# The second layer of whole expert blocks as seven block products, over halves of tokens, features and outputs

## The chip, the cores and the metric

The kernel runs on one core of a Trainium2 chip. The metric is the device time of one execution, in microseconds. Before the change it is 2567.09 us, the median of three runs from 2567.05 to 2567.15.

## The reference

An attention unit without a softmax, and behind it a layer of eight experts in which a hash of the token's number picks the expert. Everything is in float32.

```
B, S, D = 8, 2496, 256;  d_qk = 64;  N = B * S = 19968;  E, F = 8, 1024
scores = z @ z.T / S                      # per batch
x = (u * (maximum(scores, 0)**2 @ v)).reshape(N, D)
e = token_ids * 2654435761 % E            # the expert of each row
h = maximum(x @ w1[e], 0)                 # first layer, 256 -> 1024
out = h @ w2[e]                           # second layer, 1024 -> 256
```

## The kernel before

The first 1510 us or so are the attention; the change does not touch them. There each gated row of x is also stored to its slot in DRAM, where the rows of one expert stand together. What follows is the expert part, and all line numbers here are those of the kernel before.

The slots are cut into 32 **whole blocks** of 512 rows, each of one expert, and 31 **small blocks**: 27 of 128 rows of one expert, and 4 made of halves of 64 rows, three of them with two experts' weights and one, the lone half, with one. The list `work` (line 1066) takes them in turn: whole, small, whole, small, ..., and a whole one at the end. `run` (line 1016) goes through this list in steps; the program's order is written out by hand and each engine takes its instructions in that order. At step i it does the first layer of block i, and somewhere within it the second layer of block i - 1. There are two calls of `run`, since near the end a branch stands that is taken only when rows must be done again; the first call ends behind a small block.

*First layer of a whole block* (`ups_mixed`, line 872, for all but the first block; that one uses `ups`). It computes h transposed: 1024 features on partitions, 512 tokens in columns. It uses Winograd's form of Strassen's method: the weights w1 are cut into 2x2 parts over the two halves of the 256 inputs and of the 1024 features, x into 2x2 parts over inputs and tokens, and seven products of mixed parts take the place of eight. The four mixed parts of w1 (`mix_w`, line 855, s1 to s4 in `w_mix`) are made by GpSimd, the four of x (`mix_x`, line 865) by VectorE, both ahead of the block. Each product is done for two halves d of its features in PSUM banks; sums that are needed twice are copied out by ScalarE (`kept`, line 898) into one of five buffers `rest`, taken in turn, and added by VectorE (`total`, line 904); the rectification of these sums is a GpSimd instruction behind it (line 906). One of the four parts comes rectified out of PSUM by ScalarE (line 934). The eight `yield`s let `run` put other work between the pieces: at k = 1 the next small block's x is turned (`turn_x`), at k = 6 the second layer of the small block before is done.

*First layer of a small block* (`ups_of_part`, line 948): two steps of one PSUM bank each, with the tokens on partitions; ScalarE rectifies the first bank (line 944), VectorE the second (line 946), and 16 transposes on VectorE turn the result (line 982).

*Second layer* (`down`, line 984). For each 128 tokens of block i - 1 one PSUM tile of 128x256 is the sum of eight matmuls (stationary: 128 features by 128 tokens of h; moving: 128 features by 256 outputs of w2). ScalarE copies it to the SBUF (line 1005), and GpSimd issues an indirect store to the tokens' rows (line 1010). For a whole block that is four such tiles, 32 matmuls. They all stand in the second step (k = 1) of the small block's first layer, with `mix_w` for the next whole block between the second and the third of them:

```
                    for n in range(-(-len(do) * 2 // (len(banks) - k + 1))):
                        if n == 2 and work[i] >= NW:
                            mix_w(work[i + 1])
                        do.pop(0)()
```

Ahead of them in that step, and so ahead of them on VectorE, stand the rectification of the second bank, and `turn_x` and `mix_x` of the next whole block. A float32 matmul of the program stands in the trace as two records (MATMUL), each with its own weight load (LDWEIGHTS); a transpose by TensorE as one. The time from the start of one whole block to the start of the next is called a period below.

## Time and profile before

| what | value |
|---|---|
| median of 3 runs | 2567.09 us |
| the profiled execution's own time | 2569.34 us |
| its span, first to last instruction | 2567.6 us |
| TensorE busy | 2556.2 us |
| VectorE, ScalarE, GpSimd busy | 1541.3, 656.4, 1042.9 us |
| instructions | 28507 |
| granted clock of TensorE, mean | 1.000 |

Three things help to read it. The busy share is of the whole span, while the change lies in the part from about 1550 us on, so the stretches there are looked at by themselves. In the list of groups the mean is the time from an instruction's start to its end; matmuls and loads overlap with what follows, so the distance between two starts is found in the rows in order of time, as the length of a row of many minus one instruction's own, divided by their number less one. And a row in order of time gives in square brackets how long the engine had been idle before it, and who ended that.

### The profile page before, as it was taken

What the parts mean: (1) busy time and instruction counts of PE and PEld (TensorE: products, weight loads), DVE (VectorE), ACT (ScalarE), POOL (GpSimd) and SP (SyncE); (2) the same over time, 40 slices, a digit from 0 to 9 for tenths busy, and PEclk for the clock granted to TensorE, in tenths of its full rate; (3) what the DMA queues carried; (4) which work ended last, traced back from release to release, by engine and by line L of the source; (5) the groups of instructions that cost most, each with busy time, mean ns of one, the idle gap of its engine ahead of it and who ended that gap; (6) DMA issues with size and microseconds to landing.
All of it is one profiled execution on the core that took longest, in us unless ns stands there. A gap on an engine that the chain in (4) does not pass through costs nothing.

```text
span 2567.6 us, 28507 instructions
## 1 busy us (share of the span) xinstructions
PE 2556.2 (100%) x8827; PEld 1581.7 (62%) x8827; DVE 1541.3 (60%) x3441; ACT 656.4 (26%) x1392; POOL 1042.9 (41%) x980
## 2 busy tenths in 40 slices
PE   9999999999999999999999999999999999999999
PEld 4444444444444444444454457888888888888887
DVE  7976767767758758757856835444444444444443
ACT  5215204214223222232233102222222222222212
POOL 1342332332233133133231225555555555556555
PEclk9999999999999999999999999999999999999999
DMA  4442343343333333433423359667668668667651
GB/s 123 123 122 64 96 110 83 79 108 88 85 97 98 84 93 93 90 96 86 115 69 79 82 148 249 166 168 197 166 163 198 172 168 202 173 167 175 168 134 52
DMA packets 445531, 322.99 MB, mean 126 GB/s; under 512 B 267292, under 2 KB 408237, under 8 KB 445376
## 3 DMA queue, kind: packets, MB, share of 16 engines
q1 hardware_dynamic: 423456, 279.38, 44.7%
q0 software_dynamic: 20624, 41.09, 5.0%
q8 instruction: 72, 1.18, 0.2%
q14 instruction: 83, 0.68, 0.1%
q10 hardware_dynamic: 1296, 0.66, 0.1%
HBM read 231.19 MB, written 66.81 MB: 116 GB/s over the span
## 4 chain that ended last, share of the span: by engine, by line
PE 97%; issue 1%; POOL 1%; DVE 0%; POOLq 0%; ACT 0%; DVEq 0%
PE acc L362 50%; PE o_ps L991 20%; PE h_ps L889 14%; PE s_ps L235 7%; PE h_ps L976 4%; PE acc L370 2%; PE h_ps L844 1%; POOL out_dram L1010 1%; POOL hT L906 0%; DVE hT L982 0%; PE warm L655 0%; PE z_ps L179 0%; PE h_ps L957 0%; POOL u_sb L860 0%; POOL u_sb L861 0%
## 5 line engine op out<-in xcount | busy, mean ns | idle before, releaser
L362 PE MATMUL acc<-a,v_sb 128*128 128x512 f32 (+1 forms) x1760 | 765.9, 592 | 0.0
L273 DVE STREAM_TRANSPOSE m<-a 32x512 f32<-32x512 f32 (+1 forms) x896 | 603.9, 674 | 18.9 <-ACT a L251 3.6
L362 PEld LDWEIGHTS acc<-a,v_sb 128*128 128x128 f32 x1760 | 342.2, 196 | 390.5 <-issue 377.5
L362 PE MATMUL acc<-m,v_sb 128*128 128x512 f32 (+1 forms) x1280 | 527.5, 571 | 1.8 <-issue 1.8
L398 POOL TENSOR_TENSOR x_sb<-x_sb,u_sb 128x256 f32<-128x256 f32 (+1 forms) x156 | 108.3, 723 | 912.7 <-DMA x_sb<-x_way 912.7
L243 ACT ACTIVATE a<-s_ps 128x512 f32<-128x512 f32 (+3 forms) x456 | 202.1, 582 | 1036.3 <-PE s_ps L235 976.9
L362 PEld LDWEIGHTS acc<-m,v_sb 128*128 128x128 f32 x1280 | 251.1, 196 | 273.8 <-issue 271.0
L991 PE MATMUL o_ps<-m,hT 128*128 128x256 f32 (+1 forms) x1904 | 414.1, 379 | 0.0
L991 PEld LDWEIGHTS o_ps<-m,hT 128*128 128x128 f32 (+1 forms) x1904 | 353.8, 188 | 61.0 <-issue 12.5
L906 POOL TENSOR_SCALAR hT<-hT 128x512 f32<-128x512 f32 x186 | 275.1, 1496 | 96.0 <-DVE hT L905 95.0
L299 DVE STREAM_TRANSPOSE a<-a 32x128 f32<-32x128 f32 (+2 forms) x1360 | 282.3, 240 | 9.9
L1010 POOL DMA_INDIRECT out_dram<-o_sb,idx x155 | 156.3, 1009 | 320.6 <-ACT o_sb L1005 298.0
L905 DVE TENSOR_TENSOR hT<-stage,h_ps 128x512 f32<-128x512 f32 x112 | 77.0, 688 | 259.7 <-PE h_ps L889 245.5
L251 ACT ACTIVATE a<-a 128x512 f32<-128x512 f32 (+1 forms) x480 | 229.5, 639 | 0.0
L378 DVE STREAM_TRANSPOSE x_q<-acc 128x512 f32<-128x512 f32 (+1 forms) x80 | 56.7, 708 | 284.2 <-PE acc L362 281.4
L982 DVE STREAM_TRANSPOSE hT<-hT 32x256 f32<-32x256 f32 x480 | 209.0, 435 | 6.3
L1005 ACT COPY o_sb<-o_ps 128x256 f32<-128x256 f32 x158 | 58.9, 373 | 553.9 <-PE o_ps L991 553.9
L235 PE MATMUL s_ps<-zT 64*128 64x512 f32 (+1 forms) x960 | 188.7, 536 | 0.0
L889 PE MATMUL h_ps<-x_sb,u_sb 128*128 128x256 f32 x744 | 185.9, 379 | 0.0
L640 POOL DMA_INDIRECT x_rows<-x_sb,slot_i x160 | 157.2, 982 | 69.7 <-issue 36.7
L628 POOL DMA_INDIRECT slot_tokens<-token,addr x160 | 155.3, 971 | 50.8 <-issue 48.1
L235 PEld LDWEIGHTS s_ps<-zT 64*128 64x128 f32 x960 | 111.7, 186 | 93.8 <-issue 64.7
(156 smaller groups left out, 1810.9 us busy)
## 6 DMA issues: line engine op xcount, KB each, us to landing
m<-in_moe_w_dram SPq DMA_DIRECT2D x200, 256.0 KB
m<-in_moe_w_dram SPq DMA_DIRECT2D x50, 1024.0 KB
m<-stage SPq DMA_DIRECT2D x320, 64.0 KB
v_sb<-in_v_dram SPq DMA_DIRECT2D x32, 512.0 KB
u_sb<-in_u_dram SPq DMA_DIRECT2D x32, 512.0 KB
x_way<-x_q SPq DMA_DIRECT2D x128, 128.0 KB
x_sb<-x_way SPq DMA_DIRECT2D x32, 512.0 KB
v_sb<-x_rows SPq DMA_DIRECT2D x128, 128.0 KB
```

The source lines that it names most:

```text
L235: nc.tensor.matmul(ps[:, lo:n], zT[b][h, ts(t, P)], zT[b][h, ds(g * G * P + lo, n - lo)], start=True, stop=True)
L243: nc.scalar.activation(a, ps[:, lo:n], AF.Relu)
L251: nc.scalar.activation(a, a, AF.Square, scale=1.0 / S)
L273: nc.vector.transpose(o, x[ts(r, Q), 0:m * G, ts(c, Q)].rearrange("p (i s) q -> p i s q", s=G))
L299: return n * Q, lambda: nc.vector.transpose(out, in_)
L362: nc.tensor.matmul(acc[h][:, 0:queries(g)], v_sb[b][:, t, h::2], squares(b, g, t), start=(k == 0), stop=(k == TM - 1), skip_group_check=True)
L640: st = nc.gpsimd.indirect_dma_start(out=x_dram[:, :], out_offset=bass.IndirectOffsetOnAxis(ap=slot_i[0:width(c % T), c:c + 1], axis=0), in ...
L889: nc.tensor.matmul(ps[:, ts(i, W)], terms[k][0][:, ts(2 * d + i, P)], terms[k][1], start=first and i == 0, stop=True, skip_group_check=True)
L906: nc.gpsimd.tensor_scalar_max(o, o, 0.0)
L982: nc.vector.transpose(turned[ts(c, Q), :, ts(r, Q)], rows[ts(r, Q), :, ts(c, Q)])
L991: nc.tensor.matmul(ps[cols, :], hT[j][f][:, ts(t, P)][:, cols], w[:, f, :], start=(f == 0), stop=(f == n - 1), skip_group_check=True)
L1010: st = nc.gpsimd.indirect_dma_start(out=out[:], out_offset=bass.IndirectOffsetOnAxis(ap=rows, axis=0), in_=o, in_offset=None, bounds_check ...
```

## The change

The second layer of every whole block but the first is done by `downs_mixed`, again with seven products of Winograd's form. The left operand is h, cut into halves of tokens and of features; the right one is w2, cut into halves of features and of outputs. Each product is 256 tokens by 512 features by 128 outputs: eight matmuls with 128 columns, four parts of features for each of two token tiles. Products 2 and 5 or 3 share a PSUM bank; products 1, 6, 7 and 4 go to the other and add up there. ScalarE copies out three partial sums and the last part, VectorE adds the other three parts from PSUM into a whole output block (`o_blocks`), and the stores go out two at a time, behind product 3 and behind product 4.

The mixed parts of w2 are four differences on GpSimd (`mix_w2`), those of h four per half d on VectorE (`mix`), two of them with the rectification of one operand folded in. The other three parts of h are rectified in place by ScalarE (`rectify`), and GpSimd no longer rectifies. In `run`, products 1, 2, 5 and 6 stand behind the first step of the small block's first layer, products 7, 3 and 4 behind its second; `mix_w` for the next whole block keeps its condition n == 2, which now is ahead of product 4 and its stores. Two buffers of `rest` move to a new pool, since their room is taken by the mixed parts of w2.

```diff
@@ -815,6 +815,8 @@
     o_all = vpool.tile([P, T, D], F32, name="v_sb")
     nc.gpsimd.memset(o_all[:, 0:BLK // P * AHEAD + (MH - NH + 2) // 2, :], 0.0)
     xT_buf.append(turned_x(o_all, T // XW - 1))
+    assert BLK // P * AHEAD + (MH - NH + 2) // 2 <= 2 * BLK // P and T // XW > 4
+    o_blocks = [o_all[:, ts(k, BLK // P), :] for k in (2, 3)]
     w_free.append(len(w_buf))
     w_buf.append([npool.tile([P, T, NQ, Q], F32, name="zn")[:].rearrange("p t j k -> p (t j k)")[:, 0:DP * F],
@@ -850,7 +852,10 @@
     x_mix = xpool.tile([P, G, D], F32, name="x_sb")[:].rearrange("p g (k i) -> p g k i", i=Q)
     rest = [spool.tile([P, BLK], F32, name="stage")[:] for _ in range(3)]
-    rest += [xpool.tile([P, G, D], F32, name="x_sb")[:].rearrange("p g d -> p (g d)")[:, ts(k, BLK)] for k in range(2)]
+    w2_mix = [xpool.tile([P, G, D], F32, name="x_sb")[:].rearrange("p g (k d) -> p (g k) d", k=2),
+              qpool.tile([P, G * NQ, D // NQ], F32, name="x_q")[:].rearrange("p (k n) d -> p k (n d)", k=8)]
+    w2_mix = [w2_mix[k // 2][:, ts(k % 2, 4)] for k in range(4)]
+    rest += [opool.tile([P, BLK], F32, name="kept", bufs=2)[:] for _ in range(2)]
     def mix_w(j):
@@ -861,6 +866,16 @@
         nc.gpsimd.tensor_sub(s2, s1, a11)
         nc.gpsimd.tensor_sub(s3, a11, a21)
         nc.gpsimd.tensor_sub(s4, a12, s2)
+    def mix_w2(j):
+        w = w2[j][0]
+        (b11, b12), (b21, b22) = ([w[:, ts(k, FP // 2), ts(c, P)] for c in range(2)] for k in range(2))
+        t1, t2, t3, t4 = w2_mix
+        nc.gpsimd.tensor_sub(t1, b12, b11)
+        nc.gpsimd.tensor_sub(t2, b22, t1)
+        nc.gpsimd.tensor_sub(t3, b12, b22)
+        nc.gpsimd.tensor_sub(t4, b21, t2)
     def mix_x(j):
@@ -903,7 +918,21 @@
         def total(o, a, c):
             nc.vector.tensor_add(o, a, bank(c))
-            nc.gpsimd.tensor_scalar_max(o, o, 0.0)
+        def rectify(r, c, d):
+            o = part(r, c, d)
+            nc.scalar.activation(o, o, AF.Relu)
+        mixes = [apool.tile([P, 2, G, W], F32, name="hS", tag="a") for _ in range(2)]
+        h_mix[j] = [tiles[0][:, :, 0:W], tiles[1][:, :, 0:W], tiles[1][:, :, W:], *(m[:, k] for m in mixes for k in range(2))]
+        def mix(d):
+            a11, a12, a22, s1, s2, s3, s4 = (m[:, ts(d, 2)] for m in h_mix[j])
+            a21 = part(0, 1, d)
+            nc.vector.scalar_tensor_tensor(s1, a21, 0.0, a22, op0=OP.max, op1=OP.add)
+            nc.vector.tensor_sub(s2, s1, a11)
+            nc.vector.scalar_tensor_tensor(s3, a21, 0.0, a11, op0=OP.max, op1=OP.subtract)
+            nc.vector.tensor_sub(s4, a12, s2)
         begun = []
         sums = [[mm_ps.tile([P, BLK], F32, name="h_ps", tag="mm") for _ in range(3)] for _ in range(2)]
@@ -933,11 +962,75 @@
             times(d, sums[d][0], 4)
             nc.scalar.activation(part(1, 0, d), bank(sums[d][0]), AF.Relu)
-        for steps in ([(begin, 0)], [(second, 0), (sixth, 0)], [(begin, 1)], [(seventh, 0), (second, 1)],
-                      [(sixth, 1), (end, 0)], [(seventh, 1)], [], [(end, 1)]):
-            for step, d in steps:
-                step(d)
-            yield
+        mix_w2(j)
+        for steps in ([(begin, 0)], [(second, 0), (sixth, 0), (rectify, 0, 0, 0)], [(begin, 1)],
+                      [(seventh, 0), (second, 1), (rectify, 1, 1, 0)], [(sixth, 1), (end, 0), (rectify, 0, 0, 1)],
+                      [(seventh, 1)], [(mix, 0), (rectify, 1, 1, 1)], [(end, 1), (mix, 1)]):
+            for step, *at in steps:
+                step(*at)
+            yield
+    def downs_mixed(j):
+        b = w2[j][0]
+        (b11, _), (b21, b22) = ([b[:, ts(k, FP // 2), ts(c, P)] for c in range(2)] for k in range(2))
+        t1, t2, t3, t4 = w2_mix
+        a11, a12, a22, s1, s2, s3, s4 = h_mix[j]
+        terms = {1: (a11, b11), 2: (a12, b21), 3: (s4, b22), 4: (a22, t4), 5: (s1, t1), 6: (s2, t2), 7: (s3, t3)}
+        o = o_blocks.pop(0)
+        o_blocks.append(o)
+        one = acc_ps.tile([P, D], F32, name="o_ps", tag="acc")
+        both = acc_ps.tile([P, 2, D], F32, name="o_ps", tag="acc")
+        def times(ps, k, start=False):
+            for f in range(FP // 2):
+                for t in range(2):
+                    nc.tensor.matmul(ps[:, ts(t, P)], terms[k][0][:, f, ts(t, P)], terms[k][1][:, f],
+                                     start=start and f == t == 0, stop=True, skip_group_check=True)
+        def kept(ps):
+            e = rest.pop(0)
+            rest.append(e)
+            nc.scalar.copy(e[:, 0:D], ps)
+            return rows(e[:, 0:D])
+        def rows(x):
+            return x.rearrange("p (t d) -> p t d", t=2)
+        def part(r, c):
+            return o[:, ts(r, 2), ts(c, P)]
+        def send(r):
+            for t in range(2 * r, 2 * r + 2):
+                k = slots(j)[0] + t
+                store(o[:, t, :], idx[:, k:k + 1])
+        k, m, n = one[:], both[:, 0], both[:, 1]
+        times(k, 1, True)
+        e1 = kept(k)
+        yield
+        times(n, 2, True)
+        yield
+        times(m, 5)
+        nc.vector.tensor_add(part(0, 0), e1, rows(n))
+        e5 = kept(m)
+        yield
+        times(k, 6)
+        e2 = kept(k)
+        yield
+        times(k, 7)
+        nc.vector.tensor_add(part(1, 1), e5, rows(k))
+        yield
+        times(m, 3)
+        nc.vector.tensor_add(part(0, 1), e2, rows(m))
+        send(0)
+        yield
+        times(k, 4)
+        nc.scalar.copy(part(1, 0), rows(k))
+        send(1)
+        yield
+    h_mix = {}
     def relu(k, o, ps):
         if k % 2 == 0:
@@ -1019,6 +1112,10 @@
             if i < last and i + 2 < loads:
                 load_x(work[i + 2], (i + 2) % LOADS)
             do = [lambda t=t: down(work[i - 1], t, later) for t in range(slots(work[i - 1])[1])] if i > first else []
+            lower = i > first and work[i - 1] in h_mix
+            if lower:
+                steps = downs_mixed(work[i - 1])
+                do = [lambda: next(steps)] * 7
             banks = [*range(BLK // P * 2 if work[i] < NW else 2)] if i < last else []
             if first < i == AHEAD:
@@ -1038,6 +1135,9 @@
                         mix_x(work[i + 1])
                 if strassen and k == 6:
                     while do:
+                        do.pop(0)()
+                if k == 0 and lower:
+                    for _ in range(4):
                         do.pop(0)()
                 if k % 2 == 1 and not late:
                     for n in range(-(-len(do) * 2 // (len(banks) - k + 1))):
```

Three places show how instructions move. In all of them h_ps are PSUM banks of the first layer, o_ps of the second, m_..., zn and zT the expert weights as loaded, u_sb the mixed parts of w1.

GpSimd, one period late in the expert part. Before: the second pair of stores (line 1010) of a whole block, the rectifications (906) of the next with the small block's store, and then two stores, the mixing of w1 (860 to 863) and two stores.

```order
L1010 DMA out_dram<-o_sb,idx 19968x256 x2
L906 TENSOR_SCALAR hT<-hT 128x2x256 x5
L1010 DMA out_dram<-o_sb,idx 19968x256
L906 TENSOR_SCALAR hT<-hT 128x2x256
L1010 DMA out_dram<-o_sb,idx 19968x256 x2
L860 TENSOR_TENSOR u_sb<-zn 128x512
L861 TENSOR_TENSOR u_sb<-u_sb,zn 128x512
L862 TENSOR_TENSOR u_sb<-zn 128x512
L863 TENSOR_TENSOR u_sb<-zn,u_sb 128x512
L1010 DMA out_dram<-o_sb,idx 19968x256 x2
```

GpSimd in the same place after the change: the mixing of w2 (875 to 878) into x_sb and x_q, the small block's store from o_sb, two stores of the whole block's first half from v_sb, the mixing of w1 (865 to 868), two stores of the second half.

```order
L875 TENSOR_TENSOR x_sb<-m_176 128x512
L876 TENSOR_TENSOR x_sb<-m_176,x_sb 128x512
L877 TENSOR_TENSOR x_q<-m_176 128x512
L878 TENSOR_TENSOR x_q<-m_176,x_sb 128x512
L1103 DMA out_dram<-o_sb,idx 19968x256
L1103 DMA out_dram<-v_sb,idx 19968x256 x2
L865 TENSOR_TENSOR u_sb<-zn 128x512
L866 TENSOR_TENSOR u_sb<-u_sb,zn 128x512
L867 TENSOR_TENSOR u_sb<-zn 128x512
L868 TENSOR_TENSOR u_sb<-zn,u_sb 128x512
L1103 DMA out_dram<-v_sb,idx 19968x256 x2
```

The rectifications are gone, the mixing of w2 is new, and the mixing of w1 still stands between two pairs of stores; the first pair now belongs to the sums behind product 3.

VectorE, in the second step of a small block's first layer. Before: the second bank's rectification (946), turning (735) and mixing (868 to 870) the next x, the small block's transposes (982).

```order
L946 TENSOR_SCALAR hT<-h_ps 128x512
L735 STREAM_TRANSPOSE v_sb<-v_sb 128x1024
L868 TENSOR_TENSOR x_sb<-v_sb 128x512
L869 TENSOR_TENSOR x_sb<-v_sb,x_sb 128x256
L870 TENSOR_TENSOR x_sb<-v_sb,x_sb 128x256
L982 STREAM_TRANSPOSE hT<-hT 32x8x32 x16
```

After, with what each waits for: the sum behind products 1 and 2 (1015) stands ahead, those behind products 7 (1022) and 3 (1025) stand between the mixing of x and the transposes (1075).

```order
L1015 TENSOR_TENSOR v_sb<-stage,o_ps 128x2x128 [waits DMASW0_49,DMASW1_49,PE_49,Activation_49]
L1039 TENSOR_SCALAR hT<-h_ps 128x512 [waits PE_49]
L735 STREAM_TRANSPOSE v_sb<-v_sb 128x1024 [waits DMAHW2_49,DMAHW3_49,DMAHW1_49,DMAHW0_49]
L883 TENSOR_TENSOR x_sb<-v_sb 128x512 [waits DVE_49]
L884 TENSOR_TENSOR x_sb<-v_sb,x_sb 128x256 [waits DVE_49]
L885 TENSOR_TENSOR x_sb<-v_sb,x_sb 128x256 [waits DVE_49]
L1022 TENSOR_TENSOR v_sb<-stage,o_ps 128x2x128 [waits DMASW2_49,DMASW3_49,PE_49,Activation_49]
L1025 TENSOR_TENSOR v_sb<-kept,o_ps 128x2x128 [waits PE_49]
L1075 STREAM_TRANSPOSE hT<-hT 32x8x32 x16
```

The two sums have come in behind five instructions that already stood there.

TensorE, from a small block's first layer to the next whole block. Before: four matmuls of the small block (976), the 32 of the second layer (991), the next block's first products (889).

```order
L976 MATMUL h_ps<-m_179,v_sb 128x512 x4
L991 MATMUL o_ps<-m_175,hT 128x256 x32
L889 MATMUL h_ps<-v_sb,m_177 128x256 x2
L889 MATMUL h_ps<-x_sb,u_sb 128x256 x2
L889 MATMUL h_ps<-v_sb,m_177 128x256 x2
```

After: the small block's first bank (1069), products 1, 2, 5 and 6 (988), its second bank, products 7, 3 and 4, and the next block's first two products (904), the second of which reads u_sb.

```order
L1069 MATMUL h_ps<-m_177,v_sb 128x512 x2
L988 MATMUL o_ps<-m_176,hT 128x128 x16
L988 MATMUL o_ps<-x_sb,hS 128x128 x16
L1069 MATMUL h_ps<-m_177,v_sb 128x512 x2
L988 MATMUL o_ps<-x_q,hS 128x128 x8
L988 MATMUL o_ps<-m_176,hS 128x128 x8
L988 MATMUL o_ps<-x_q,hT 128x128 x8
L904 MATMUL h_ps<-v_sb,zn 128x256 x2
L904 MATMUL h_ps<-x_sb,u_sb 128x256 x2
```

The second bank has moved from ahead of the second layer into its middle, with 24 short matmuls behind it.

## Rows read from the trace of the kernel before

**Rows 1.** The page: busy times, the chain that ended last, two groups.

```profile
PE 2556.2 (100%) x8827; PEld 1581.7 (62%) x8827; DVE 1541.3 (60%) x3441; ACT 656.4 (26%) x1392; POOL 1042.9 (41%) x980
...
PE 97%; issue 1%; POOL 1%; DVE 0%; POOLq 0%; ACT 0%; DVEq 0%
...
L362 PEld LDWEIGHTS acc<-a,v_sb 128*128 128x128 f32 x1760 | 342.2, 196 | 390.5 <-issue 377.5
...
L251 ACT ACTIVATE a<-a 128x512 f32<-128x512 f32 (+1 forms) x480 | 229.5, 639 | 0.0
```

**Rows 2.** The chain in order of time, one period: start us, us, what.

```profile
2007.57 10.36 PE h_ps L889 x48
2017.93 3.45 PE o_ps L991 x16
2021.39 1.73 PE h_ps L889 x8
2023.11 3.43 PE h_ps L976 x8
2026.55 13.81 PE o_ps L991 x64
```

**Rows 3.** Stretch of 100 us: PE, PEld, DVE, ACT, POOL busy, PEclk, DMA, GB/s.

```profile
2000.00:2100.00 100.00, 100.00 (x442) 83.51 (x441) 45.86 (x88) 21.88 (x43) 57.05 (x46) 1.00 0.65 163
```

**Rows 4.** In order of time, TensorE and its loads: start us, us, what.

```profile
4.69 2.46 PE L179 MATMUL z_ps<-ident,zn 128*128 128x128 f32 x21
...
1444.88 0.31 PEld L362 LDWEIGHTS acc<-a,v_sb 128*128 128x128 f32 x2
...
1927.57 0.30 PEld L991 LDWEIGHTS o_ps<-m,hT 128*128 128x128 f32 x2 [0.81 <-issue]
...
2026.38 13.98 PE L991 MATMUL o_ps<-m,hT 128*128 128x256 f32 x64
```

**Rows 5.** Groups by form, TensorE and loads: busy us, mean ns.

```profile
L179 PE MATMUL z_ps<-ident,zn 128*128 128x128 f32 x21 | 2.5, 273 | 0.0
...
L991 PEld LDWEIGHTS o_ps<-m,hT 128*128 128x128 f32 x1824 | 346.3, 190 | 57.5 <-issue 11.5
```

**Rows 6.** In order of time, VectorE, behind a small block's second bank.

```profile
2026.59 0.69 DVE L946 TENSOR_SCALAR hT<-h_ps 128x512 f32<-128x512 f32 x1 [3.61 <-PE h_ps L976]
...
2028.46 0.69 DVE L868 TENSOR_TENSOR x_sb<-v_sb 128x512 f32<-128x512 f32 x1
...
2029.65 0.42 DVE L870 TENSOR_TENSOR x_sb<-v_sb,x_sb 128x256 f32<-128x256 f32 x1
2029.99 7.17 DVE L982 STREAM_TRANSPOSE hT<-hT 32x256 f32<-32x256 f32 x16
```

**Rows 7.** In order of time, GpSimd's stores and mixing, and one VectorE sum.

```profile
2007.59 0.99 POOL L1010 DMA_INDIRECT out_dram<-o_sb,idx  x1 [0.15 <-issue]
...
2008.88 0.97 POOL L1010 DMA_INDIRECT out_dram<-o_sb,idx  x1 [0.30 <-issue]
...
2034.14 0.98 POOL L1010 DMA_INDIRECT out_dram<-o_sb,idx  x1 [2.41 <-ACT o_sb L1005]
2035.13 1.29 POOL L860 TENSOR_TENSOR u_sb<-m 128x512 f32<-128x512 f32 x1
...
2347.45 0.41 DVE L997 TENSOR_TENSOR o_sb<-o_sb,o_ps 64x256 f32<-64x256 f32 x1 [1.53 <-ACT o_sb L996]
...
2348.15 0.95 POOL L1010 DMA_INDIRECT out_dram<-o_sb,idx  x1 [0.59 <-DVE o_sb L997]
```

**Rows 8.** Groups by form, the other engines: busy us, mean ns.

```profile
L870 DVE TENSOR_TENSOR x_sb<-v_sb,x_sb 128x256 f32<-128x256 f32 x31 | 14.8, 476 | 1.1
...
L997 DVE TENSOR_TENSOR o_sb<-o_sb,o_ps 64x256 f32<-64x256 f32 x1 | 0.4, 413 | 1.5 <-ACT o_sb L996 1.5
...
L1005 ACT COPY o_sb<-o_ps 128x256 f32<-128x256 f32 x158 | 58.9, 373 | 553.9 <-PE o_ps L991 553.9
...
L906 POOL TENSOR_SCALAR hT<-hT 128x512 f32<-128x512 f32 x186 | 275.1, 1496 | 96.0 <-DVE hT L905 95.0
```

## The prediction

> **What bounds the kernel now.** Read three views, in this order. The page's busy shares and its chain of work [rows 1]: TensorE is busy for 2556.2 of 2567.6 us, and the chain that ended last is TensorE for 97% of the span. So the kernel is bound by what TensorE has to stream, and any wait that is put on TensorE is added to the time. Next the table by stretches [rows 3]: in the expert part TensorE fills 100 of 100 us at a granted clock of 1.00 (2.4 GHz), VectorE 46, ScalarE 22, GpSimd 57. So work moved to the other three has room, if it is done in time. Last the chain in order of time [rows 2], for one period of the expert part, a whole block and a small one: 10.36 us of first-layer products, 3.45 for the small block's second layer, 1.73 for the rest of the first layer, 3.43 for the small block's first layer, 13.81 for the whole block's second layer; 32.78 us, piece behind piece, with no gap.
>
> **What is taken away.** The whole block's second layer is 32 products, two TensorE records each, 64 records of 256 columns in 13.81 us [rows 2], 0.216 each. Now it is seven products of eight matmuls with 128 columns: 112 records. No row has this form (128 rows, 128 columns, accumulating). Its nearest rows are the transposes at the start: 21 records of 128 columns and 128 rows, each with its own weight load, from the first start to the last end 2.46 us; one lasts 273 ns [rows 4, 5], so they start (2.46 - 0.27) / 20 = 0.109 us apart. That is half of 0.216 and a little, and I take it. From above, three rows bound it: where two loads of this very line follow each other with no matmul to hide under, the pair takes 0.30 us and one takes 0.19, so the second starts 0.11 behind the first; in the attention, at 0.196 a load [rows 1], the same sum gives 0.31 - 0.196, 0.115 [rows 4]; and a load of this line is recorded as 0.190 us long [rows 5]. The first two say that loads just keep pace with 128 columns. The last is a load's length, not its pace: of the two that start 0.11 apart each is drawn that long; it is a rival below. So 112 x 0.109 = 12.25 us, 1.56 less per block; 31 blocks (all but the first, which keeps the old form): 48 us.
>
> **What is added off TensorE.** Per period GpSimd loses six rectifications of 1.50 us [rows 8] and gains four differences of w2 at 1.29, as its other mixing [rows 7], 9.0 less and 5.2 more. They are queued at the start of the block's first layer, behind the mixing of w1 and two stores (below): done some 14 us into the block, and product 5 wants the first of them after 20.8 (10.36 + 3.45 + 1.73 + 1.72 for the small block's first bank + 3.5 for two products). ScalarE gains four rectifications within the SBUF, 0.64 each by the squares [rows 1]; its four copies of 0.37 [rows 8] stay in number. VectorE gains eight sums of 128x512, 0.7 each [rows 6], and three of 128x256, 0.41 each [rows 8], 6.8 us beside the 15 per period it has now. The last four sums must come ahead of product 5. Count from the end of the last product 3 of the first layer: VectorE adds (0.21 after TensorE, as between matmul and rectification in [rows 4, 6], then 0.7) and mixes, s1 by 1.6 us. TensorE meanwhile has product 4 (0.86), the small block's first bank (1.72), products 1 and 2 (3.5): 6.1. ScalarE's last rectification is there at 0.86 + 0.21 + 0.64 = 1.7, and product 2 wants it at 4.3. So all of this is hidden with 2.6 us to spare; even at twice its length it costs nothing, and without that cover it would be 2.8 us a block. Loads and their queue on SP keep their order; the weights of w2 are asked for more than a block ahead, and a GpSimd wait for them would meet an engine with time. These parts together: 0.
>
> **What is added on TensorE: the path to the next block.** The order on GpSimd changes: the mixing of the next block's w1 stood between the second and third of four single stores, 5 us ahead of the end of the second layer (it starts at 2035.13, the next block at 2026.55 + 13.81 = 2040.36 [rows 2, 7]). Now it stands behind two stores, and these wait for the sum behind product 3, the last but one. Follow it from the moment at which the small block's second bank ends on TensorE and product 7 begins (before: 2026.38 [rows 4]).
> VectorE starts the rectification 0.21 later, turns the next x and mixes it, and is free at 2029.99, that is at 3.61 [rows 6]. In the old order only the 16 transposes came then; now two sums stand behind this chain, those of products 7 and 3, each 0.41 (the nearest is a 64x256 sum from PSUM [rows 8]): 4.02 and 4.43. From a VectorE sum to a store is 0.28 (2347.45 + 0.41 to 2348.15 [rows 7]): 4.71. Two stores in a row start 1.29 apart, and the mixing starts 0.99 after a store [rows 7]: 6.99. The first mixed sum takes 1.29 [rows 7]: 8.28. Then 0.1 for the signal (an estimate, half of the 0.21 above) and 0.11 for a weight load with nothing above it [rows 4]: 8.49.
> TensorE needs that sum for the second product of the next block. It gets there after products 7, 3 and 4 (48 records, 5.25) and the first product (4 records of 0.216, 0.86): 6.11. So it stands still for 2.38 us: some 0.7 of it ahead of product 4, which overwrites what the sum of product 7 reads (4.02 + 0.2 against 3.50), and 1.7 ahead of the second product of the next block. In the old order the same sum was ready at 2036.4, more than 4 us early. The further sums come 1.3 us apart and are wanted 1.7 or more apart, so nothing waits a second time.
> Net, per ordinary period: -1.56 + 2.38 = **+0.82 us**. Everything that shortens TensorE's three products only lengthens the wait, since the chain hangs on VectorE and GpSimd.
>
> **The sum.** Of 31 blocks 28 are ordinary: +23.0. The block beside the lone half (whose second step holds no matmul) has product 7 right behind product 6 and waits for its copy, 0.21 + 0.37 + 0.2 = 0.78, and for the mixing 2.05 (the chain is 0.32 shorter): -1.56 + 0.78 + 2.05 = +1.3. The block ahead of the program's break has the small block's second layer behind the mixing, and only the wait of 0.7: -0.9. The last block waits 0.78 and ends with two stores, not one, 1.29 more: +0.5. Together +23.9. The profiled execution took 2569.34 us, of which 2567.6 is its span; the median of the runs is 2567.09, 2.25 below it, and the profile's cost is the same on both sides: 2569.34 + 23.9 - 2.25 = **2591 us**, 0.9% slower.
>
> **Its bounds.** Short end of the chain: sums 0.34 apart, as 2029.65 stands to 2029.99 [rows 6], stores 1.14 apart (the gap of 0.15 in [rows 7]) and no 0.1: 8.1, net +0.4, 2579. Long end: sums of 0.48 [rows 8], stores 0.1 longer each (an estimate; 0.95 to 0.99 in [rows 7]): 8.8, net +1.1, 2600. A record of 0.115 adds 64 x 0.006 = 0.4 per block (only the 64 records ahead of the chain count), 2611.
>
> **A rule that speaks against the change.** At 128 rows the loads and matmuls of the second layer start every 0.216 us, and each load of 0.190 lies beside the matmul ahead of it [rows 2, 5]; one after the other, at 0.11 a load, they could not start closer than 0.32. The Trainium skill, "TensorE: Matmul & The Clock Gate", Part 3, The mechanism, says that a load overlaps matmuls in flight only when its row group differs. Here all row groups are the same and they overlap, so the trace disagrees at 256 columns; no row shows it at 128 columns outside the transposes.
>
> **The rivals.** (a) *The loads are not hidden under short matmuls.* A record then costs the load's recorded 0.190: 21.3 us a block, 7.5 more than before; the three products become longer (48 x 0.19 + 0.86 = 10) than the chain, so no wait is left. 31 x 7.5 = 232: 2799. If load (0.11) and streaming (0.109) follow each other outright, it is 0.22 a record: 2900. The rule just named would give the latter. For: no row of the form. Against: transposes at 0.109 with a load each, and the pair of loads at 0.11. Together 5%.
> (b) *The stores don't hold GpSimd for as long as they are drawn.* Its spans are rough; if a store only hands over its addresses and the next instruction can begin beside it, the 2.28 us of two stores go from the chain: ready at 6.2, TensorE there at 6.11, and the gain of 1.56 a block stands nearly whole: 2567 - 45 = 2522. It decides at a chain of 7.67, 0.82 shorter than worked out: there the kernel is as fast as before. For: spans on GpSimd are said to be rough. Against: the mixing at 2035.13 starts right at the end of the store from 2034.14, and two stores keep 1.29 apart [rows 7]. Faster by over 0.2% wants 7.5 or less: 11%.
> (c) *It cancels.* A chain between 7.5 and 7.85: 7%.
> (d) *The change doesn't do what it says*, because the sums s1 to s4 or the copies come late: worked out above with 2.6 us to spare; 1%, slower: without the cover 2.8 more a block, 2680.
>
> **Chances.** The forecast 76%, (a) 5, (b) 11, (c) 7, (d) 1. Slower by over 0.2% (5 us, about what a measurement of this kernel can tell from no change) 0.82, within it 0.07, faster 0.11. The range reaches from 2567, which takes in the slower half of (c), to 2611, the long end with slow records; (a), (b), (d) and the other half of (c) stay outside, some 20%.
>
> **What will show it.** In the changed profile: 16 records of a product in 1.75 us plus one latency; on TensorE two waits per period, some 0.7 for VectorE ahead of product 4 (line 988) and 1.7 for GpSimd at line 904, in the list of waits 29 times each; GpSimd going store, store, mixing without a gap; VectorE and ScalarE waiting, never waited for elsewhere; a period of 33.6 us. It is wrong if the mixing starts before the first of the two stores ends, if records start more than 0.115 apart, or if the granted clock drops below 1.00 behind the waits, which no row here can show.

## The result, and the profile after

| | before | after |
|---|---|---|
| median of the runs (4 each) | 2567.12 us | 2602.59 us (2602.26 to 2603.89) |
| ratio | | 1.0138, 95% interval 1.0121 to 1.0156 |
| span of the profiled execution | 2567.6 us | 2600.6 us |

The kernel became 1.4% slower. The forecast was 2591 us, within 2567 to 2611. The page of the changed kernel, where [rows 1] stand before:

```profile
span 2600.6 us, 32201 instructions
...
PE 2534.7 (97%) x10315; PEld 1594.6 (61%) x10315; DVE 1756.2 (68%) x3782; ACT 724.6 (28%) x1516; POOL 922.3 (35%) x918
```

TensorE is busy 21.5 us less and the span is 33.0 us longer. The stretch of [rows 3] after the change (columns as there):

```profile
2000.00:2100.00 100.00, 95.17 (x575) 82.40 (x574) 63.99 (x116) 28.13 (x54) 44.77 (x39) 1.00 0.67 166
```

The clock is at its upper level (2.4 GHz) and TensorE is idle for 5 of 100 us, in three periods. The list of waits from 1560 to 2470 us (us in total, times, longest) says where; line 904 is line 889 of before, line 988 holds the new products, and PEld is TensorE's weight loads, which wait for the same sum:

```profile
PEld h_ps L904 <- POOL u_sb L865: 43.3, 27, 2.1
...
PE h_ps L904 <- POOL u_sb L865: 32.5, 27, 1.7
...
PE o_ps L988 <- DVE v_sb L1022: 10.9, 26, 0.4
```

Both waits are those of the forecast. One period in order of time, the columns as in [rows 4, 6, 7]:

```profile
2036.89 3.73 PE L988 MATMUL o_ps<-m,hT 128*128 128x128 f32 x32
...
2045.76 1.95 PE L988 MATMUL o_ps<-x_q,hS 128*128 128x128 f32 x16
...
2045.96 0.69 DVE L1039 TENSOR_SCALAR hT<-h_ps 128x512 f32<-128x512 f32 x1 [3.03 <-PE h_ps L1069]
2046.57 1.23 DVE L735 STREAM_TRANSPOSE v_sb<-v_sb 128x1024 f32<-128x1024 f32 x1
...
2049.36 0.41 DVE L1022 TENSOR_TENSOR v_sb<-kept,o_ps 128x256 f32<-128x256 f32 x1
...
2049.69 0.41 DVE L1025 TENSOR_TENSOR v_sb<-kept,o_ps 128x256 f32<-128x256 f32 x1
...
2049.92 2.02 PE L988 MATMUL o_ps<-x_q,hT 128*128 128x128 f32 x16 [0.43 <-DVE v_sb L1022]
...
2050.38 0.97 POOL L1103 DMA_INDIRECT out_dram<-v_sb,idx  x1 [15.09 <-DVE v_sb L1025]
2051.66 0.98 POOL L1103 DMA_INDIRECT out_dram<-v_sb,idx  x1 [0.30 <-issue]
...
2052.66 1.28 POOL L865 TENSOR_TENSOR u_sb<-m 128x512 f32<-128x512 f32 x1
...
2053.99 1.13 PE L904 MATMUL h_ps<-x_sb,u_sb 128*128 128x256 f32 x4 [1.18 <-POOL u_sb L865]
```

Read it downwards. The second bank ends and product 7 begins at 2045.76; VectorE rectifies it, turns and mixes x, and only then adds (2049.36, 2049.69); product 4 waits 0.43 for the first of these sums. The store waits for the second, the mixing of w1 (line 865) for two stores, and the second product of the next block 1.18 for the mixing.

From start to start of whole blocks in the two traces, the time went here:

| part | forecast | measured |
|---|---|---|
| ahead of the first changed block | 0 | -1.6 |
| the first period | -0.8 | +1.3 |
| 26 ordinary periods | +21.7 | +22.3 |
| period at the lone half | +0.9 | +1.0 |
| period ahead of the program's break | +0.8 | **+9.0** |
| period behind the break (block 60) | -0.8 | -2.1 |
| last block to the end | +2.2 | +3.1 |
| sum | +23.9 | +33.0 |

The forecast gave each wait to the block whose second layer causes it. From start to start, the wait ahead of the next block's second product (1.66 forecast) falls into the next period, and the column counts it there: the first period and the one behind the break hold no such wait, the last block does. The terms and their sum are those of the prediction.

An ordinary period is 33.60 us, 32.79 before: +0.81. The miss lies at the break, 8.2 us; the other rows miss by 2.1, 0.6, 0.1, -1.3, 0.9 and -1.6, and nearly cancel. The break before (the small block's second layer follows the whole block's, 80 records in a row, with the transposes beside them), and after:

```profile
2483.35 17.43 PE L991 MATMUL o_ps<-m,hT 128*128 128x256 f32 x80
...
2486.95 7.17 DVE L982 STREAM_TRANSPOSE hT<-hT 32x256 f32<-32x256 f32 x16
```
```profile
2518.89 0.41 DVE L1025 TENSOR_TENSOR v_sb<-stage,o_ps 128x256 f32<-128x256 f32 x1
...
2519.11 2.02 PE L988 MATMUL o_ps<-x_q,hT 128*128 128x128 f32 x16 [0.43 <-DVE v_sb L1022]
2519.22 7.17 DVE L1075 STREAM_TRANSPOSE hT<-hT 32x256 f32<-32x256 f32 x16
...
2526.49 6.39 PE L1084 MATMUL o_ps<-m,hT 128*128 128x256 f32 x16 [5.35 <-issue]
```

and the same after, by stretches:

```profile
2519.00:2527.00 8.00, 2.54 (x17) 2.36 (x18) 7.18 (x17) 0.37 (x1) 6.94 (x6) 0.88 0.10 34
2527.00:2533.00 6.00, 5.88 (x16) 4.39 (x14) 0.00 (x0) 0.09 (x1) 1.96 (x2) 0.59 0.57 137
```

The small block's 16 transposes (7.17 us) now come behind the two sums, and only product 4 is left beside them. The small block's second layer, which reads what they write and in an ordinary period comes some 12 us behind product 4, follows at once here: it waits 5.35 us, until 0.1 us behind the end of the transposes (2526.39; the row itself names no releaser), the granted clock falls (0.88, then 0.59 on average between its two levels), and 16 records that take 3.62 elsewhere (at 2030.00, same form) take 6.39.

### The profile page after: what moved, and what is told of

Same layout as the page of the kernel before. It is cut to its first block, busy times and chain, and to the rows that moved or that the text cites. A ratio compares the mean times of both kernels' runs of the same rounds, so it can differ in the third digit from the quotient of the medians.

```text
span 2600.6 us, 32201 instructions
## 1 busy us (share of the span) xinstructions
PE 2534.7 (97%) x10315; PEld 1594.6 (61%) x10315; DVE 1756.2 (68%) x3782; ACT 724.6 (28%) x1516; POOL 922.3 (35%) x918
## 5 line engine op out<-in xcount | busy, mean ns | idle before, releaser
L1103 POOL DMA_INDIRECT out_dram<-v_sb,idx x125 | 122.5, 980 | 481.1 <-DVE v_sb L1025 456.2
L904 PEld LDWEIGHTS h_ps<-x_sb,u_sb 128*128 128x128 f32 x744 | 138.9, 190 | 67.6 <-POOL u_sb L865 46.5
L988 PE MATMUL o_ps<-x_sb,hS 128*128 128x128 f32 x992 | 115.8, 275 | 0.0
L1084 PE MATMUL o_ps<-m,hT 128*128 128x256 f32 (+1 forms) x496 | 109.3, 386 | 5.3 <-issue 5.3
L988 PEld LDWEIGHTS o_ps<-x_sb,hS 128*128 128x128 f32 x992 | 113.3, 192 | 0.0
```

Source lines behind the costliest of these rows:

```text
L904: nc.tensor.matmul(ps[:, ts(i, W)], terms[k][0][:, ts(2 * d + i, P)], terms[k][1], start=first and i == 0, stop=True, skip_group_check=True)
L988: nc.tensor.matmul(ps[:, ts(t, P)], terms[k][0][:, f, ts(t, P)], terms[k][1][:, f], start=start and f == t == 0, stop=True, skip_group_che ...
L1103: st = nc.gpsimd.indirect_dma_start(out=out[:], out_offset=bass.IndirectOffsetOnAxis(ap=rows, axis=0), in_=o, in_offset=None, bounds_check ...
```

## The experiments

My theory for the ordinary period: the chain from the second bank through VectorE's sums, two stores and the mixing sets the next block, and TensorE's records cost 0.11 each. The rivals: short records are slower, or some other engine is late. Times below are medians beside the kernel before on the same chip.

**The record alone.** The kernel before, its second layer cut into matmuls of 128 columns for 31 blocks, no other change:

```diff
+                if 0 < j < NW:
+                    for c in range(2):
+                        nc.tensor.matmul(ps[:, ts(c, P)], hT[j][f][:, ts(t, P)], w[:, f, ts(c, P)],
+                                         start=(f == c == 0), stop=True, skip_group_check=True)
+                    continue
```

> The kernel before, with each matmul of the second layer of the 31 whole blocks cut into two of 128 columns: 128 records per block where 64 were, the same work and the same order. It prices the short record by itself. At the 0.109 us of the prediction: 128 x 0.109 = 13.95 against 13.81, 2567.1 + 31 x 0.14 = 2571. At the 0.1115 that 32 records in 3.73 us of the changed kernel give: 14.27, 2581. At the recorded length of a load, 0.190: 24.3, 2892.

Measured: 2582.87 us, 33.27 a period where it was 32.79. 128 records replace 64 of 13.81 us, so one costs (13.81 + 0.48) / 128 = 0.1116. A record is not held to its load's recorded 0.19: rival (a) is out.

**One link of the chain at a time.** First the mixing of w1 ahead of the stores, then the next tokens turned and mixed at the small block's first bank, then both:

```diff
-                        if n == 2 and work[i] >= NW:
+                        if n == (0 if lower else 2) and work[i] >= NW:
```
```diff
-                if k == (banks[-1] if i < AHEAD else 0 if i == AHEAD else 1) and AHEAD <= i + 1 < max(last, loads):
+                if k == (banks[-1] if i < AHEAD else 0 if i == AHEAD or lower else 1) and AHEAD <= i + 1 < max(last, loads):
```

> The changed kernel with one thing moved: the mixing of the next block's w1 on GpSimd comes ahead of product 7, and so ahead of the two stores behind product 3. Theory of the queue (the wait ahead of the next block's second product is GpSimd's order): that wait of 1.45 us per period goes, the wait of 0.66 ahead of product 4 stays; 2602.6 - 29 x 1.45 = 2560, and a period of 32.1 us. Rival, VectorE's late sums hold everything: hardly a change, 2595 or more. Rival, the short matmuls themselves cost it: no change, 2602.

> The changed kernel with another thing moved: turning and mixing the next x on VectorE comes in the small block's first step, ahead of the sums of the second layer. Theory of one chain (the two waits are one, since the mixing of w1 follows the sum behind product 3): the wait ahead of product 4 goes, but product 3 itself then sets that sum, only 0.25 us earlier than now, and the wait ahead of the next block's second product grows from 1.45 to about 1.85; 2602.6 - 29 x 0.25 = 2595. Rival, two waits that stand by themselves: 0.66 per period less, 2583.

> Both moves together. Theory of one chain: both waits go, 2.11 us per period; a period of 31.5 us, 2602.6 - 29 x 2.11 = 2541, below the kernel before by 1%. What is left above 2567 - 31 x 1.32 = 2526 is the stretch at the program's break. If the saving of seven products were not there at all, it would be no faster than the kernel before, 2567.

| | time | ratio | ordinary period |
|---|---|---|---|
| mixing first | 2580.59 us | 1.0051 (1.0034 to 1.0068) | 32.67 |
| tokens first | 2603.08 us | 1.0143 (1.0126 to 1.0159) | 33.44 |
| both | 2599.08 us | 1.0123 (1.0106 to 1.0140) | 33.03 |

Tokens first showed that it is one chain: product 4's wait was gone, the wait for the mixing grew from 32.5 to 45.8 us in 27 times, and the ordinary period fell by 0.16 us, near the 0.25 expected. The time did not fall with it (2595 expected), since the period at the lone half grew from 32.4 to 36.5 us. Mixing first took the wait for GpSimd away, but uncovered another: 32.67 a period instead of 32.1. Its waits in the same stretch as above:

```profile
PE o_ps L988 <- DVE v_sb L1022: 11.2, 27, 0.4
PEld h_ps L904 <- ACT stage L916: 11.2, 17, 0.7
...
PE h_ps L904 <- ACT stage L916: 4.4, 17, 0.3
...
PE h_ps L904 <- ACT kept L916: 2.3, 9, 0.3
```

ScalarE now comes late with the next block's copies (line 916): its first rectification in place waits for a VectorE sum, that one for the 16 transposes, and the copies are queued behind it. Both together should have been best, and I was wrong by 58 us: some 40 of them in the 26 ordinary periods (33.03, not 31.5), 8.5 at the lone half (40.9 us, 32.4 in the changed kernel; what waits there stays open). In that run, GpSimd's mixing (POOL) and VectorE's mixing of h in order of time:

```profile
2027.73 1.85 DVE L932 SCALAR_TENSOR_TENSOR hS<-hT 128x512 f32<-128x512 f32 x1
2027.74 1.29 POOL L865 TENSOR_TENSOR u_sb<-m 128x512 f32<-128x512 f32 x1
...
2029.10 1.61 POOL L866 TENSOR_TENSOR u_sb<-u_sb,m 128x512 f32<-128x512 f32 x1
...
2029.62 1.64 DVE L933 TENSOR_TENSOR hS<-hS,hT 128x512 f32<-128x512 f32 x1
2030.67 1.72 POOL L867 TENSOR_TENSOR u_sb<-m 128x512 f32<-128x512 f32 x1
2031.18 1.76 DVE L934 SCALAR_TENSOR_TENSOR hS<-hT 128x512 f32<-128x512 f32 x1
...
2032.35 1.71 POOL L868 TENSOR_TENSOR u_sb<-m,u_sb 128x512 f32<-128x512 f32 x1
```

The two slow each other, as if in turns: VectorE's sums of 0.69 take 1.64 to 1.85, mixing of 1.27 takes 1.61 to 1.72, one of each in about 1.65, and VectorE is late for everything behind it. The Trainium skill, "SBUF — State Buffer", Who interferes with whom, has this rule: a VectorE instruction with two SBUF inputs and a GpSimd instruction that reads the SBUF exclude each other. The rows agree; VectorE's sums with one operand in PSUM kept their 0.42 beside the same mixing (below).

**Keeping them apart, and the rectification.** In the run with both, one more GpSimd instruction ahead of the mixing reads an element of the second layer's first sum, so that the mixing starts behind VectorE's sums; and, with the mixing first alone, ScalarE's first rectification moved behind the next two copies:

```diff
+                            if lower:
+                                nc.gpsimd.tensor_copy(w_mix[0][:, 0:1], o_blocks[-1][:, 0, 0:1])
```
```diff
-                      [(second, 0), (sixth, 0), (rectify, 0, 0, 0)], [(begin, 1)],
+                      [(second, 0), (sixth, 0)], [(begin, 1), (rectify, 0, 0, 0)],
```

> The changed kernel with the mixing of the first layer's weights ahead of the stores and the turning and mixing of the next tokens at the small block's first bank, as in the run with both (2599.1 us, 33.03 a period), and with one instruction more: GpSimd copies one element of the second layer's first sum ahead of its mixing, so that the mixing starts only behind VectorE's sums of the first layer and its mixing of tokens. Theory (the two engines slow each other when both work on two tiles in SBUF: 0.69 to 1.75 and 1.27 to 1.7 us): kept apart, VectorE's sums take 0.69 again, the two waits on ScalarE's copies shrink to the 0.66 a period of the run that moves the mixing alone, and the period is about 32.1, the time about 2562. Rival (VectorE is late by its queue, whatever GpSimd does): the period stays at 33.0 and the time at 2599.

> The changed kernel with the mixing ahead of the stores (2580.6 us, 32.67 a period), and ScalarE's first rectification in place of the next block put behind the copies of its next two banks instead of ahead of them. Theory (that rectification waits for a sum of VectorE, which is behind 16 transposes, and holds the copies behind it): the wait of 0.66 a period for a kept bank goes, the period is about 32.0, the time about 2561. Rival (the copies are late by themselves, or the next sum takes the place of the wait): 32.4 to 32.7 a period, 2572 to 2581.

Measured: with the hold 2574.84 us (1.0031, 1.0019 to 1.0043), 32.51 a period: 0.52 better, less than the 0.9 expected, since the wait on ScalarE's copies stayed at some 0.8 a time. With the rectification moved 2563.60 us (0.9987, 0.9978 to 0.9996), 32.15 a period, near the expected 32.0: of the waits only product 4's 0.4 is left. So each is a cause of its own. In that second run the two engines still slow each other, and no wait comes of it:

```profile
2013.56 1.84 DVE L932 SCALAR_TENSOR_TENSOR hS<-hT 128x512 f32<-128x512 f32 x1
```

In these runs their slowing cost time only where the tokens, too, are queued ahead of VectorE's sums. All four repairs in one, with a first attempt at the break that puts the transposes right behind their bank and all seven products behind them; and that attempt alone:

```diff
-                if k == 0 and lower:
+                ends = i + 1 == last < len(work)
+                if k == 1 and ends:
+                    next(up, None)
+                if k == 0 and lower and not ends:
```

> All four repairs on the changed kernel: mixing of the first layer's weights ahead of the stores but held until VectorE's sums are done, tokens of the next block mixed at the small block's first bank, the first rectification behind the next two copies, and the transposes ahead of the break behind their bank. Theory (these are all the waits there are, and TensorE is left with the records alone, 1.32 us a block fewer): the period is about 31.5, the break's about 38.5, the time 2602.6 - 28 x 2.1 - 8 = about 2536, faster than the kernel before by 31. Rival (a wait that these hid, on the stores or on a buffer, takes their place): 32.0 to 32.7 a period, 2550 to 2572.

> The changed kernel, with one step altered: at the small block ahead of the program's break the 16 transposes are issued right behind that block's bank, and all seven products of the whole block before it behind them. Theory (this period grew by 9.04 us because the transposes, 7.17, had only one product of 2.02 left beside them, so that the small block's second layer waited 5.35 us and then ran in 6.39 us at a granted clock of 0.59): the wait and the fall of the clock both go, 5.35 + 2.8 = 8.1 us, the period falls from 46.6 to about 38.5, and the time from 2602.6 to about 2594.5. Rival (the growth lies in the break itself, in the stores or in the drain behind it): the period stays at 46 to 47 and the time at 2602.

With all: 2548.06 us (0.9927, 0.9913 to 0.9940), the ordinary period 31.48, as expected; there TensorE has no wait left. The hold (line 1149) and what it keeps whole:

```profile
2012.40 0.18 POOL L1149 COPY u_sb<-v_sb 128x1 f32<-128x1 f32 x1 [7.80 <-DVE v_sb L1015]
2012.66 1.26 POOL L865 TENSOR_TENSOR u_sb<-m 128x512 f32<-128x512 f32 x1
...
2014.00 1.26 POOL L866 TENSOR_TENSOR u_sb<-u_sb,m 128x512 f32<-128x512 f32 x1
...
2015.23 1.27 POOL L867 TENSOR_TENSOR u_sb<-m 128x512 f32<-128x512 f32 x1
...
2016.45 1.27 POOL L868 TENSOR_TENSOR u_sb<-m,u_sb 128x512 f32<-128x512 f32 x1
...
2017.11 0.42 DVE L1022 TENSOR_TENSOR v_sb<-kept,o_ps 128x256 f32<-128x256 f32 x1 [1.15 <-PE o_ps L988]
...
2032.38 0.69 DVE L933 TENSOR_TENSOR hS<-hS,hT 128x512 f32<-128x512 f32 x1
```

But the break took 47.2 us in it and 47.9 in the attempt alone (2604.80 us, 1.0147, 1.0132 to 1.0163), where 38.5 was expected in both. The row there, in the attempt alone:

```profile
2516.19 7.17 DVE L1075 STREAM_TRANSPOSE hT<-hT 32x256 f32<-32x256 f32 x16
2523.40 0.42 DVE L1015 TENSOR_TENSOR v_sb<-kept,o_ps 128x256 f32<-128x256 f32 x1
...
2524.64 3.67 PE L988 MATMUL o_ps<-x_q,hS 128*128 128x128 f32 x16 [8.03 <-ACT stage L994]
```

The transposes now stood ahead of the first sum; ScalarE's copies waited for that sum, and product 7 for them, 8.03 us (the mixed parts that it reads, x_q with hS, are those of product 7; the expectation below that names product 6 is wrong there), with slow records behind (3.67 for 16, at a granted clock of 0.50). The wait had only been moved. Two more ways, each alone and with the other repairs (there, tokens are turned as before where the small block is the lone half): four products with the first sum ahead of the transposes and three behind (the edit is shown); then 4 of the 16 transposes ahead of that sum and 12 behind (a `yield` behind every four transposes lets `run` take them in parts).

```diff
+                ends = i + 1 == last < len(work)
-                if k == 0 and lower:
+                if k == (1 if ends else 0) and lower:
                     for _ in range(4):
                         do.pop(0)()
+                if k == 1 and ends:
+                    next(up, None)
```

> The changed kernel, with only the step ahead of the program's break altered, another way than in the last attempt (which put the transposes ahead of the first sum and moved the wait of 8.0 us to product 6): both banks of the small block first, then the whole block's first four products with the first sum, then the 16 transposes (7.17), then the last three products with the other sums. Behind the first sum TensorE has products 5, 6, 7 and 3, 4 x 1.95 = 7.8 us, beside the transposes. Theory (the period grew because the transposes had only 2.02 us of records beside them; cover them and the wait of 5.35 and the 2.77 of slow records behind it go): the period falls from 46.6 to about 38.5, the time to about 2594.5. Rival (wherever the transposes stand, something waits for VectorE, or the break itself holds TensorE): 44 to 47 and 2600 to 2603.

> The kernel with all repairs (2548.1 us, 31.48 a period, 47.2 at the break, 34.5 at the block that meets the lone half) with the break done in the new way, and the next tokens turned at the second bank again where the small block is the lone half. Theory: the break's wait of 7.2 us and the 2.8 of slow records behind it go, 47.2 to about 37.2; the lone half gives back about 2.1; the time is about 2548.1 - 10.0 - 2.1 = 2536. Rival (the break holds TensorE, as above): 45 to 47 there, 2546 to 2548.

> The changed kernel with the step ahead of the break as in the last attempt (42.4 us there, 2600.0), but 4 of the 16 transposes ahead of the first sum and 12 behind it. That attempt gave back 4.2 of 8.1 us: its first sum began 1.9 us later than reckoned, because it waits for product 5 as well as product 2, VectorE was idle for those 1.93, the transposes and the second sum came as much later, product 4 waited 2.0 us for that sum, and its 16 records took 3.65 instead of 1.95. Theory: with the idle time filled by 4 transposes (1.8 us) that wait and the slow records go, 42.4 - 2.0 - 1.7 = 38.7, the time about 2596.3. Rival (something else than the transposes' place holds the end of this step, such as a buffer or the break): 42 to 43 and 2600.

> The kernel with all repairs (2536.9 us, 40.4 at the break) with 4 transposes ahead of the first sum and 12 behind it there. Theory: product 4's wait of 2.1 us goes, the period is about 38.3 and the time about 2534.8. Rival: 40 to 41 and 2537.

| break as in | alone: break, time, ratio | with the repairs: break, time, ratio |
|---|---|---|
| the change | 46.6, 2602.59 us, 1.0138 | |
| 4 products ahead | 42.4, 2600.00 us, 1.0133 | 40.4, **2536.87 us, 0.9882** (0.9865 to 0.9898) |
| and 4 transposes ahead | 40.0, 2605.87 us, 1.0136 | 38.5, 2539.23 us, 0.9883 (0.9867 to 0.9900) |

The last two rows' runs were on different chips (before: 2567.31 and 2570.38 us), so the ratios are to be compared. The step itself is confirmed: it gave back 4.2, then 6.7 of the 9.0 us as the transposes got more beside them. The first of these ways:

```profile
2511.28 3.74 PE L988 MATMUL o_ps<-x_sb,hS 128*128 128x128 f32 x32
2513.33 0.42 DVE L1015 TENSOR_TENSOR v_sb<-kept,o_ps 128x256 f32<-128x256 f32 x1 [1.93 <-PE o_ps L988]
2513.67 7.17 DVE L1075 STREAM_TRANSPOSE hT<-hT 32x256 f32<-32x256 f32 x16
...
2520.87 0.42 DVE L1022 TENSOR_TENSOR v_sb<-kept,o_ps 128x256 f32<-128x256 f32 x1
...
2521.43 3.65 PE L988 MATMUL o_ps<-x_q,hT 128*128 128x128 f32 x16 [2.00 <-DVE v_sb L1022]
```

The first sum waits for product 5 as well as for product 2, 1.9 us more than reckoned; product 4 then waits 2.00, and again runs slowly (3.65, at a granted clock of 0.50 to 0.51). With four transposes in that idle time it waits 0.32 and takes 2.02. Yet the time did not follow, alone: the next period grew from 30.5 to 35.4. The reason, in that run:

```profile
2536.15 0.98 POOL L1104 DMA_INDIRECT out_dram<-o_sb,idx  x1 [0.30 <-issue]
...
2546.02 1.25 POOL L1104 DMA_INDIRECT out_dram<-v_sb,again  x1 [8.89 <-ACT hT L924]
...
2552.87 0.98 POOL L1104 DMA_INDIRECT out_dram<-v_sb,idx  x1 [0.30 <-issue]
2553.87 1.28 POOL L875 TENSOR_TENSOR x_sb<-zT 128x512 f32<-128x512 f32 x1
...
2555.20 5.02 PE L988 MATMUL o_ps<-x_sb,hS 128*128 128x128 f32 x28 [4.24 <-POOL x_sb L875]
```

GpSimd's six stores that the program holds over until behind the branch began 8.9 us behind the store ahead of them, 6.8 in the run before; the mixing of w2 is queued behind them, and TensorE waited 4.24 for it. What held GpSimd there is not the releaser that the row names, which had ended at 2543.98, but an instruction of the program: `nc.gpsimd.drain()` stands ahead of the branch in every one of these kernels (line 1180 here, 1074 in the kernel before). Its row in that run (min, median and longest in ns, first and last start):

```profile
L1180 POOLq DRAIN  x1: 12098/12098/12098, 2533.1 to 2533.1; - x1
```

It ends at 2545.16, and the next store begins 0.86 behind it. What it waits for shows in the stores ahead of it: in the ten kernels whose trace has the landing of the last of these, the drain ends 1.65 us behind that landing. In this run the last packet of that store ended at 2543.14, 7.0 us behind the store's start, where it was 4.9 in the run before (there the drain ends at 2538.82). The weights' loads filled the DMA engines meanwhile (share 0.89 from 2536 to 2544); that they made the store land later is likely, but was not tested. With the repairs the mixing of w1 comes ahead of the stores there, and the next period is 30.4; but two periods near the start, which this edit leaves alone, took 0.6 more each, so no gain can be told between the two.

The best kernel is 1.2% faster than the one before and 2.5% faster than the change (0.9882 / 1.0138). Its stretch from 2000 to 2100 us:

```profile
2000.00:2100.00 100.00, 100.00 (x603) 86.61 (x602) 67.08 (x125) 29.55 (x57) 46.31 (x43) 1.00 0.66 171
```

## Why the prediction was right, and where not

The mechanism of the ordinary period came as forecast, and nearly to the digit. That 2602.6 us still lies within 2567 to 2611 is luck: the upper end was worked out for a longer chain and slower records, and neither came; the break used up that room.

- *The pace of a record.* Taken 0.109. In the row at 2036.89, 32 records take 3.73 us, one alone 0.275, so (3.73 - 0.275) / 31 = 0.1115, and the cut-up kernel gives 0.1116. It lies inside the bounds, 0.109 to 0.115. A block saves 13.81 - 112 x 0.1115 = 1.32, not 1.56. The rule that was weighed (the Trainium skill, "TensorE: Matmul & The Clock Gate", Part 3, The mechanism) does not hold here: loads recorded as 0.19 us long in one row group lie beside 128-column matmuls too.
- *The chain on VectorE and GpSimd.* Right link by link: VectorE free at 3.60 (2045.76 to 2049.36; forecast 3.61), sums 0.33 apart and not 0.41, stores 1.28 apart, the mixing behind them. The two waits cost 2.12 a period together (33.60 - 31.48, the period without waits), forecast 2.38: taken from start to start, 0.67 and 1.44 by the rows (product 4 starts 2.38 behind product 3, and the next block 1.86 behind product 4, where products start 1.78 apart; likewise at line 904); the idle times in brackets, 0.43 and 1.18, are smaller, since a row's drawn length reaches past the start of the next. Both terms were too large by a quarter of a microsecond, and cancel: -1.32 + 2.12 = +0.80, forecast +0.82, measured +0.81. Half of that had to cancel, as the prediction says: slower records of the last three products (48 x 0.0025 = 0.12 us) only shorten the wait. The other half is luck: the 64 records ahead cost 0.16 more, and the chain, shorter by closer sums, gave about as much back.
- *The stores hold GpSimd.* They do: the mixing starts at 2052.66, behind the store from 2051.66 (0.98). Rival (b) is out, and (c) with it.
- *Everything else hidden, at no cost.* True as long as the chain is longer. Hidden below it were 0.5 a period behind ScalarE's first rectification, which no step of the prediction looked at, and the slowing of VectorE by GpSimd. In the first period the copies behind that rectification held TensorE for 3.02 us (1554.14, line 904; a wait of 1.08 stood near there before), most of the 2.1 between the measured +1.3 and the forecast -0.8; in the run with the rectification moved it is gone. Also, VectorE's sum at 2030.87 in the changed kernel took 1.36 beside the mixing of w2, with nobody waiting. The cover that I counted held: VectorE's mixing of h was done at 2037.92, product 5 began at 2040.46.
- *The block ahead of the break: the step that failed.* I wrote "only the wait of 0.7, -0.9". I had looked at the mixing there, not at the transposes, which the change moved behind the sums, and at who waits for them when no next block comes between. They lost their cover: 5.35 of wait and 2.77 of slow records (6.39 instead of 3.62). From start to start that forecast is +0.8, measured +9.0, and these two make 8.1 of the 8.2 between them. The text named a clock that falls behind a wait as what could make it wrong, but gave it no price.
- *The last block*: forecast +0.5, or +2.2 with the wait at its start, measured +3.1. Four stores stand in a queue 1.28 apart behind the last sums (first at 2592.71, last at 2596.56), where I counted one extra.
- *Block 60* got 2.15 faster, where the forecast from start to start is 0.8: before, its second layer waited 1.44 for rectifications queued behind the stores held over the branch; they are on ScalarE now. I had not looked there.
- *From span to median.* I took 2.25 us off as the profile's cost, the same on both sides. The changed kernel's profiled execution took 2602.26, its median is 2602.59: no such cost. In all thirteen kernels but the one before, the profiled execution lies between 0.65 below and 1.6 above the median, so it looks like the scatter of one execution; 2.25 of the miss of 11.6.

## What to carry to other kernels

When TensorE is full, price a faster algorithm by what it asks of the other engines in the last microseconds ahead of a hand-over, and follow each queue there to the end: the saving here was 1.32 us a block, the reordered queues took 2.12. A repair uncovers the next wait, so work out which engine is late next before expecting the whole gain; the mixing moved alone still lost 0.5%, with the rectification moved as well it gained 0.1%, and all the moves together turned +1.4% into -1.2%. Look at each place where the loop's pattern ends, since a cover that a step has in every period can be missing there. And when an engine sits idle and the releaser that its row names does not fit, look for an instruction of its sequencer, such as a drain, by its line.

## What the runs showed of the hardware

- Float32 records of 128 rows and 128 columns, each with its own load, stream at 0.1115 us, half of 256 columns (0.216) and 3% more.
- VectorE sums with both inputs in the SBUF and GpSimd sums slow each other when they meet: 0.69 grew to 1.64 to 1.85 and 1.27 to 1.61 to 1.72 us, about 1.65 for one of each.
- A drain on GpSimd ended 1.65 us behind the landing of the last indirect store ahead of it, in all ten kernels that show this landing; it lasted from 5.4 to 12.1 us at the break of the fourteen kernels.
- Behind a TensorE wait of 5.35 or 8.03 us, and in one place behind one of 2.00, the clock was granted at the lower level (1.2 GHz; 0.50 to 0.51 in these stretches) for the next records: 16 of 256 columns took 6.39 instead of 3.62 (behind 5.35), 16 of 128 columns 3.67 (behind 8.03) or 3.65 (behind 2.00) instead of 1.95. Behind a wait of 2.10 in the best kernel they took 2.02, but behind the next one, 2.16, the first four records took 1.21 and the next four 1.91 instead of 1.03. Which waits bring it on, these runs do not settle.
